# W' = w3 · w_out in three float32r passes instead of float32, its depth sum cut in two, and all float64 chunks converted by three VectorE operations

## The chip, the cores and the metric

One core of a Trainium2 chip. The metric is the device time of one execution in microseconds, the median of several runs. Engines: PE (TensorE, matmuls; PEld its weight loads), DVE (VectorE), ACT (ScalarE), POOL (GpSimd), SP (SyncE, which only issues DMAs here). Each works through its own queue in order.

## What is computed

Clustered attention over 2 x 8 heads of 768 x 64: a query sees only the keys whose nearest centroid is the same. Two MLPs follow on the 1536 x 512 result.

```python
scores = np.where(mask, scale * np.matmul(q, k.transpose(0, 1, 3, 2)), -1000000000.0)
attn = np.exp(scores - np.max(scores, axis=-1, keepdims=True))
attn = attn / (np.sum(attn, axis=-1, keepdims=True) + 1e-09)
x = np.matmul(attn, v)                                   # then to 1536 x 512
h = x @ w_in                                             # 512 x 2048
x = np.where(h >= 1, h, np.where(h <= -1, 0, (h + 1) ** 2 / 4)) @ w_out
out = ((x @ w1) * (x @ w2) @ w3) @ w_out2                # w1, w2 512 x 1024; w3 1024 x 1024; w_out2 1024 x 512
```

All weights arrive as float64. Because nothing stands between the last two products, the kernel makes W' = w3 @ w_out2 (1024 x 512) once, beside the attention, and multiplies by W'.

## The kernel before, in words

**Order.** Every step is registered with `add` (name, engines that can take it, planned cost, function, needs). ORDER is a string of letter pairs; each is the number of a step and which of its engines takes it, and the steps are emitted in that order. "takes", "frees", planned costs and due times were used when the string was made; at run time they emit nothing.

**Course.** Attention of batch 0 runs beside W' and the conversion of the first weights (to about 200 us); then the MoE products of batch 0 beside the attention of batch 1 (to about 470 us); then the products of batch 1. One score tile goes through PE (L855, two products in float32r), DVE (maximum, L863), POOL (scale, L868), ACT (exp, L876), PE (transpose, L893), ACT or DVE (copy to `pt`). Four PSUM tiles `sc` serve this in batch 0, `av` holds a PV product, and one bank `mo` serves W' and the transposes of the reciprocals (L950). Score tiles and head pairs are counted from 0.

**Chunks.** A weight chunk is 128 x 512. `chunk` (L1093) loads its float64 words (`w64`), and builds a float32 in a buffer `wf` (a ring of four): ACT takes the absolute of the high words (L1110), DVE clamps (L1114); then, in every second chunk (`by_add`), DVE shifts (L1136) and puts sign and top bits back (L1142), ACT rounds the low words (L1148), and POOL adds them (L1152). In the others ACT scales the low words by another form (L1120), and DVE ors them in while shifting (L1124) and ors the sign (L1130): three DVE operations, none on POOL. A chunk used by a float32r product is split into high and low halves: `whi` (ACT or DVE, L348 or L350), `wlo` (POOL or DVE, L353). 72 chunks are float64: 8 of w_out2, 16 of w3, and 48 that are also kept in DRAM (`wd`) for batch 1. The first 40 are all of w_out2 and w3 and 16 of the rest.

**W'.** For each of eight row blocks m and both halves hf of the depth, `wp_mm` (L1208) multiplies a w3 chunk, straight from `wf` in float32, by four blocks of `wo2` (float32, in SBUF), both halves into the one `mo` bank (L1212). After the second half `wp_copy` takes the bank to a `wf` buffer, and `wp_put` to DRAM. The eight steps with hf = 0 and those with hf = 1 alternate.

Of the kernel before, what the change touches and what calls it, by code (L numbers as in the profile page):

```python
# [38 lines left out]
    "###%$V$.$2$0#*#,#0$X$4$]$Z%s%X%Z#.:m%V#(#2%c#4$6%r%e%k$_$H%|%h:|&#&%$8$:$a%y%_&,#m#L;.%]$<$>$q$c%m$@$J$D$e$F"  # L39
    "%a#6#a#e#P;<%u:o$s$g#Z$i$B$L$k#F;H%i:q%o$m:s)u$N:w:u%w#:$#:y#V#H#8;#;()w#g#c$o$u#_#i#@#X;0#y)y)|;8#u#w$w#B*#"  # L40
    "#q;X*%$P;%#>$y$|;*;,;2;R;>$R$T*(**#R#o;g#]*4*,%#&*;B;4*.;_&)$,#T;6;@;:*6;J*@*B#s$%;Z*0;i*8#N*:;L;N*L#|;k*D*F"
    "*<;D#k;m*2;F*>*H#<;]#J#D*N;u;q*X;o*P*J$($**Z;a*R*]*u<(*_+(*T;P;T;w;c;e*a*W;|*c*e*g+4*w<6*m<*;s<B+*<2&0*y+6+,"
    "*|&5&3<R&>+.;y<,+8+:<.<#+L+#<8<%+0<<+<+%<:&7*i+2+@<0*k<D+X+B<4;V<T+N<e+D<X*o+P+F+Z+R*r+]&/+_+H+T*s+>&=+J+V+u"
    "+a+e<V<><F<H+c,4&:<Z,(+w&8<g+m,*+y<u<o<@,,+|,6<i<J,8,:,#<],.<k<_,L<L<N<m,&=*&F<|,0,<,@+g<P,B=:<q<w,N,2,P<y,>"
    "=#=%,D,R,X&H=L<b,F<c,u,w=,=(+i+k%>=.,Z,H,T=]%%<s,]%(,y=0=4=2=@=6,_,|,a,K,W=V-#+o=<=N=>=B-4&c=Q-(+r-%=k,c=8-*"
    "-,-6&D=c=|=_+s-8-:=D=a=e-.=R&U-@&@&B=F-0-<=g=i=I,e&L,m-2-B-D=J&N-?&K,g-F,i&R&Y=u=T&W>(=m-H-X,l=X,o=o-L-K&P&_"
    "-N-P-Z=Z>4>D>R-R-],r=q=s&e-_&^-u=w>>%B>#-w-T-a&b-y>c-V>%=y>J>*-|.#,s>6-d>,>8>F>T>.-e.(>]-g>:-m.*>u.%&k>H.,>L"
    "..>N>V>X><>0&g-i&[>2>@.4%*>P.@-l.L.6%@?,>Z.8>i.0>B.B.D.:.N>_.2&n&r.P&i.F.<.R&u-o>e?%.X.Z.H>a>w.]?:>y>|._&p?#"
    "?(-q.J?J.>>q.T.V>g>k>m>s.u.a?2/4.w?.>o/(&y?0?*?]/6.c.y.|&|/*(%()?m/,&w/@/#/./0($(-?P?D-s?<?4%,.m%D/B?>?L?_?@"
    "/8/:/<?a?6.e?8.g?N?R/%%./2?T/>?c?V?B%F%0?o?s?|%2?g/D?F?H/F/H@2?q%4(*?e%H?i%J?X/L?u/J?Z.i/N/X@D.k&s%L/P?k@,/Z"  # L50
    "/R/T%6/]?w%N@#/_?y@T(.@&.o.r%8/a/V/c%P.s@c@8%:@(/u@*@4/m%<%R%T@.@F@V@s/w/y/e(4@6@:@N0(@<04@H/|0#@JA,@>0608@Z"
    "0@@L@00*0:0,@P0&0B0.000D@m0<@A/g/i0F0LA<0H@X@]@e03@_0X/k@g@a@B0N@R0>@i0P0J0Z/o@kAJ0R0]0u@yA60T0w@u@o@qA.@w0y"
    "A>@|0|/r0_AB0a0WA#A%A@ALAD0cAFAH(01(/s(20eA0AZ1#1L0g1*0m1,1.10ANAP1NA2AT1%ARAVA4A(A*(612A81416180iF4FP1@Aa0l"
    "1X(81:1PA:1Z1B1]1_1D0o(;1<(=1FA]1H1RAmA_AX(>Ac1J(EAe(BAg1>(A1e1g(M(H1TAi0q1a1W(NAk1i1c2*(GAo0sB21kAq1u2,(J1m"
    "BP1w2.201y1|(P(Z22(RB424B61o2#2%1r1s26(T2(Bo(VAsAuAw(X282:BRBTB%B(Ay2F(]B82<2H2JC42>2A2LBc2BB+B,B:A|B=2DBr2N"
    "BDB#2PCRCqBeB>2RBg2TB/B1C7F>BsC(C9BFBiFkB@BH2cBB2V2XBV2eBJ2g2ZC*BM2]2_C-BuBk2iBNCU2aBm2kC.BXCV3%3(2mBZBw3*D%"
    "C0B]2oByC:34D4B|B_BaCFC<363,C$C&CtCXC33.C>Cu30DBCHC@3238D(D*3BCJCe3:CL3D3FCZDP3=3HCw3>Cg3@3P(a(`D7C]D93RCBCD"
    "2yCi3JC_Ck3L3N3T3V(g(c2qC|3XCyCNCQCnD,3_(e3Z3]DE3mD.D#DFDoCp3a(i3o3cE42s(t3q3eD>D@ER(l(u(m3s3gD:D<3i3u2uD04>"
# [1728 lines left out]
```

## Time and profile before

| | us |
|---|---|
| median of 3 runs (lowest to highest) | 735.21 (732.62 to 736.18) |
| the profiled execution's own time | 729.0 |
| its span, first to last instruction | 727.3 |
| PE busy in it | 706.3 |
| DVE busy in it | 620.3 |
| ACT busy in it | 467.9 |
| POOL busy in it | 308.2 |

The profile is of one execution, and its time need not be the median of the others. Busy shares are averages over stages that work differently, so the stretches of the attention, which has all engines at work, are to be read by themselves. An instruction's duration contains its start-up, which overlaps the one ahead of it: on a full queue the distance from start to start is shorter.

### The profile page before, as it was taken

The numbers are of one execution on the slowest core, as the hardware profiler recorded it, in microseconds if no ns is written. First come the engines' busy times: TensorE is split into PE (matmuls) and PEld (weight loads), VectorE is DVE, ScalarE is ACT, GpSimd is POOL, SyncE is SP. The second block draws the span as 40 slices with busy tenths as digits, with TensorE's granted clock in tenths as the row PEclk, the third lists the DMA queues.
The fourth block names the chain that finished last, engine by engine and source line by source line (L and its number), as shares of the span: only waits on it lengthen the run. The fifth ranks groups of instructions, "written<-read, shape, count | busy, mean of one in ns | idle before, by whom it ended". The sixth has DMA issues, their size and how long they took to land.

```text
span 727.3 us, 11952 instructions
## 1 busy us (share of the span) xinstructions
PE 706.3 (97%) x4120; PEld 620.5 (85%) x4121; DVE 620.3 (85%) x1120; ACT 467.9 (64%) x872; POOL 308.2 (42%) x371
## 2 busy tenths in 40 slices
...
GB/s 297 119 205 135 252 202 228 178 271 118 223 236 147 187 181 230 213 228 244 165 242 216 228 244 157 189 185 132 56 74 89 44 73 59 73 59 73 59 64 80
DMA packets 120204, 117.37 MB, mean 161 GB/s; under 512 B 80400, under 2 KB 89040, under 8 KB 120144
## 3 DMA queue, kind: packets, MB, share of 16 engines
...
q8 instruction: 32, 0.52, 0.3%
...
## 4 chain that ended last, share of the span: by engine, by line
PE 86%; DVE 5%; DMA 4%; ACT 3%; issue 2%; POOL 0%; ACTq 0%; POOLq 0%; DVEq 0%
PE mo L1268 34%; PE sc L1521 9%; PE sc L855 8%; PE mo L1212 6%; PE sc L1268 6%; PE mo L1521 6%; PE sc L893 4%; PE av L964 4%; PE av L972 3%; PE av L1521 2%; PE av L1268 2%; DMA vn<-phl 1%; DMA pt<-phl 1%; DMA wd<-wf 1%; DVE nm L863 1%
## 5 line engine op out<-in xcount | busy, mean ns | idle before, releaser
L1268 PE MATMUL mo<-X,whl 128*128 128x384 f32 x912 | 168.0, 338 | 0.0
L1268 PEld LDWEIGHTS mo<-X,whl 128*128 128x128 f32 x912 | 158.6, 188 | 2.5 <-issue 0.9
L1268 PE MATMUL mo<-G,whl 128*128 128x384 f32 x696 | 129.1, 340 | 0.8 <-DVE X L353 0.8
L1268 PEld LDWEIGHTS mo<-G,whl 128*128 128x128 f32 x696 | 122.3, 188 | 2.8 <-DVE X L353 1.1
L863 DVE TENSOR_REDUCE nm<-sc 128x1 f32<-128x768 f32 x96 | 90.1, 951 | 17.3 <-PE sc L855 13.1
L353 POOL TENSOR_TENSOR whl<-wf,whl 128x512 fp32r<-128x512 f32 x50 | 65.4, 1309 | 60.0 <-ACT whl L348 35.6
L1152 POOL TENSOR_TENSOR wf<-wf,w 128x512 int32<-128x512 int32 x32 | 45.0, 1408 | 56.9 <-DVE wf L1142 18.1
L868 POOL TENSOR_SCALAR nm<-nm 128x1 f32<-128x1 f32 x96 | 29.7, 310 | 92.0 <-DVE nm L863 88.7
L348 ACT ACTIVATE whl<-wf 128x512 fp32r<-128x512 f32 x71 | 44.6, 628 | 29.0 <-PE mo L1268 10.0
L855 PE MATMUL sc<-k,q 128*128 128x512 f32 (+1 forms) x192 | 54.8, 367 | 4.0 <-DVE kq L586 1.4
L1212 PE MATMUL mo<-wo,wf 128*128 128x512 f32 x128 | 57.9, 595 | 0.0
L876 ACT ACTIVATE sc<-sc,nm 128x768 f32<-128x768 f32 x44 | 38.3, 870 | 26.4 <-POOL nm L868 25.3
L876 ACT ACTIVATE P<-sc,nm 128x768 f32<-128x768 f32 x52 | 46.4, 896 | 13.0 <-DVE nm L863 7.0
L855 PE MATMUL sc<-kq 80*128 80x512 f32 (+1 forms) x192 | 49.4, 338 | 0.0
L353 DVE TENSOR_TENSOR phl<-sc,phl 128x768 f16<-128x768 f32 x44 | 41.8, 951 | 8.2 <-ACT phl L348 7.9
L893 PEld LDWEIGHTS sc<-ident,P 128*128 128x128 f32 x312 | 35.3, 140 | 12.2 <-ACT P L876 3.6
L1110 ACT ACTIVATE wf<-w 128x512 f32<-128x512 f32 x64 | 41.6, 671 | 4.2 <-POOL whl L353 2.3
L1212 PEld LDWEIGHTS mo<-wo,wf 128*128 128x128 f32 x128 | 23.3, 190 | 24.0 <-issue 23.0
L893 PE MATMUL sc<-ident,P 128*128 128x128 f32 x312 | 41.2, 274 | 1.8 <-ACT P L876 1.0
L855 PEld LDWEIGHTS sc<-k,q 128*128 128x128 f32 x192 | 31.4, 189 | 11.9 <-issue 3.9
L353 POOL TENSOR_TENSOR wh<-ws,wh 128x256 fp32r<-128x256 f32 x42 | 31.3, 758 | 17.8 <-DVE wh L350 9.6
L348 ACT ACTIVATE pt<-sc 128x768 f32<-128x768 f32 (+1 forms) x40 | 31.8, 811 | 9.7 <-PE sc L893 7.4
(242 smaller groups left out, 1546.4 us busy)
## 6 DMA issues: line engine op xcount, KB each, us to landing
...
```

The lines of the kernel that those rows point to most:

```text
L348: nc.scalar.activation(out=out, in_=in_, func=AF.Copy)
L353: (nc.gpsimd if e == "POOL" else nc.vector).tensor_tensor(out=out, in0=a, in1=b, op=ALU.subtract)
L855: nc.tensor.matmul(ps[:, n], q[0:n_rows, q0:q0 + 128], k[0:n_rows, n], start=first, stop=not first)
L863: nc.vector.tensor_reduce(out=nm, in_=T[("sc", b), s], axis=AX.X, op=ALU.max, negate=True)
L868: nc.gpsimd.tensor_scalar(out=tl[s, "nm"], in0=tl[s, "nm"], scalar1=SCALE, scalar2=EC, op0=ALU.mult, op1=ALU.add)
L876: nc.scalar.activation(out=new(("P", b), s).rearrange("p n s -> p (n s)") if by_pe(s) else T[("sc", b), s], in_=T[("sc", b), s], func=AF.E ...
L893: nc.tensor.transpose(T[("sc", b), s][:, c], p[:, c], ident)
L1110: nc.scalar.activation(out=T["wf", i], in_=T[w64, i].bitcast(F32)[:, :, 1], func=AF.Abs, scale=1.0 if by_add else float(2.0 ** 16))
L1152: nc.gpsimd.tensor_tensor(out=w, in0=w, in1=T[w64, i].bitcast(I32)[:, :, 0], op=ALU.add)
L1212: nc.tensor.matmul(acc, w[:, k4 * 128:(k4 + 1) * 128], wo2[:, hf * 4 + k4], start=(hf == 0 and k4 == 0), stop=(hf == 1 and k4 == 3),)
L1268: nc.tensor.matmul(acc, w[:, a, k4 * 128:(k4 + 1) * 128], rhs(c, k4), start=(first and k4 == 0 and n == 0), stop=(last and k4 == 3 and n = ...
L1521: nc.tensor.matmul(ps, lhs(av, a, k), rhs(bv, c, k), start=k == 0 and n == 0, stop=k == 1 and n == 2,)
```

## The change

- W' is made of high and low halves in float32r, three passes (high x high, high x low, low x high), as the other products are. So the 8 chunks of w_out2 and the 16 of w3 are split (24 `whi`, 24 `wlo`).
- The depth sum is cut in two: all eight first halves come first. `wp_part` copies each from the bank to a `wf` buffer, `wp_keep` writes it to DRAM (`wp0`), `wp_back` reads it again, and `wp_add` (DVE) adds the second half from the bank; `wp_put` is as before.
- Of the split w_out2 blocks six lie in four buffers, two of which are used twice; blocks 0 and 1 lie in the part of `X0` that the outputs of head pairs 2 and 3 fill later.
- `by_add` is False: all 72 float64 chunks take the three DVE operations, and POOL's addition is gone from 36 of them (20 of the first 40).
- ORDER is new, with some steps given to another engine.

The diff without the ORDER strings and some unchanged lines:

```diff
     down = const.tile([128, 1], F32, name="down")
+    wp0 = dram.tile([KF2, 128, DM], F32, name="wp0")
     wp = dram.tile([DM // 128, 128, KF2, 128], F32, name="wp")
...
     kq0 = early_p.tile([128, 2, NP, S], F32, name="kq0")
-    wo2 = early_p.tile([128, KF2, DM], F32, name="wo2")
+    BUFS["wo2"] = [early_p.tile([128, 2, DM], F32R, name=f"wo2{i}") for i in range(KF2 // 2)]
+    RINGS["wo2"] = KF2 // 2
+    BUFS["wo2x"] = [X0[:, :, j, :DM] for j in (KD - 1, KD - 2)]
+    RINGS["wo2x"] = 2
     late = {}
...
         "c_load": ((0.45, 0.18),), "al": ROWS, "ul": ROWS, "vl": ROWS, "ap": ROWS, "vT": ((0.62, 2.7),),
-        "sT": ((0.62, 2.7),), "k2": ROW * 2 + MASK, "wps": ((0.45, 1.05),), "wd": ((0.45, 1.05),),
+        "sT": ((0.62, 2.7),), "k2": ROW * 2 + MASK, "wps": ((0.45, 1.05),), "wps0": ((0.45, 1.05),), "wpl": ((0.45, 1.05),), "wd": ((0.45, 1.05),),
         "xs": ROW, "xr": ROW, "os": ROW,
...
                     [(("sc", b), s)],
-                    [((x, b), (u, h)) for x in ("k1", "q1", "kq2")] if t == NQ - 1 and g == NG - 1 else [],
+                    [((x, b), (u, h)) for x in ("k1", "q1", "kq2")],
                     near=(("sc", b), s),
...
                 ("pv", u, g), {"PE": 4.1 if whole(u) else 3.13}, p, pv(u, g), [("vT", u)] + [("sT", s + r) for r in range(NS)],
-                [("av", (u, g))], [("pt", (u, g, 0)), ("pt", (u, g, 1))] + ([("vn", u)] if g == NG - 1 else []), near=("av", (u, g)),
+                [("av", (u, g))], [("pt", (u, g, 0)), ("pt", (u, g, 1)), ("vn", u)], near=("av", (u, g)),
             )
...
             if b == 0:
-                add_split("x", nm, p + 3.5, lambda a, j=j, g=g: X0[:, a, j, cols(g)], [("xm", u, g)], "av", (u, g))
+                add_split("x", nm, p + 3.5, lambda a, j=j, g=g: X0[:, a, j, cols(g)], [("xm", u, g)] + ([("wp", m, 0) for m in range(KF2)] if j >= KD - 2 else []), "av", (u, g))
             else:
...
     nchunk = [0]
-    N_EARLY = 2 * KF2 + wo2.shape[1] + AHEAD
+    N_EARLY = 3 * KF2 + AHEAD
     c64 = []
...
-    def chunk(t, src, is64, split=True, dst=None, needs=(), keep=None):
+    def chunk(t, src, is64, split=True, halves="whl", needs=(), keep=None):
         i = nchunk[0]
...
         w64 = ("w64", 0 if i < N_EARLY else 1)
-        by_add = low_by_pool(i)
+        by_add = False
...
         def absv(e):
-            if dst is None:
-                new("wf", i)
-            else:
-                T["wf", i] = dst
+            new("wf", i)
             nc.scalar.activation(out=T["wf", i], in_=T[w64, i].bitcast(F32)[:, :, 1], func=AF.Abs, scale=1.0 if by_add else float(2.0 ** 16))
...
         def hi(e):
-            copy(e, new("whl", i)[:, 0], T["wf", i])
+            copy(e, new(halves, i)[:, 0], T["wf", i])
...
         def lo(e):
-            w = T["whl", i]
+            w = T[halves, i]
             sub(e, w[:, 1], T["wf", i], f(w)[:, 0])
...
             add(("wl", i), {"ACT": 0.2}, t - 14.0, load, list(needs) + W_AFTER[i:i + 1], [(w64, i)], behind="w64", moves=((0.46, 1.8),))
-            add(("wabs", i), {"ACT": 0.56}, t - 9.0, absv, [("wl", i)], [] if dst is not None else [("wf", i)], behind="wf")
+            add(("wabs", i), {"ACT": 0.56}, t - 9.0, absv, [("wl", i)], [("wf", i)], behind="wf")
             add(("wc", i, 0), {"DVE": 0.34, "POOL": (1.92, LATE)}, t - 8.6, clamp, [("wabs", i)])
...
         if split:
-            add(("whi", i), {"ACT": 0.52, "DVE": (0.34, LATE)}, t - 5.0, hi, [last], [("whl", i)], behind="whl")
+            add(("whi", i), {"ACT": 0.52, "DVE": (0.34, LATE)}, t - 5.0, hi, [last], [(halves, i)], behind=halves)
             add(("wlo", i), {"POOL": 1.3, "DVE": (0.61, LATE)}, t - 4.0, lo, [("whi", i)], frees=[("wf", i)])
...
-    W_ACC = [("mo", 0), "av", ("sc", 0), ("sc", 0)][:W_SIDE] + [("mo", 0)] * (KF2 - W_SIDE)
-
-    def wp_acc(m, first=False):
-        ring, name = W_ACC[m], ("wp", m)
-        t = new(ring, name) if first else T[ring, name]
-        if ring == ("sc", 0):
-            o = 0 if where[ring, name] % PER[0] == 0 else S - 512
-            t = t[:, o:o + 512]
-        return t
-
-    def wp_mm(i, m, hf):
-        def fn(e):
-            w = T["wf", i]
-            acc = wp_acc(m, hf == 0)
+    def wo2_home(kt):
+        return "wo2x" if kt < 2 else "wo2"
+
+    def wp_mm(i, m, hf, x):
+        def fn(e):
+            w, acc = T["whl", i], new(("mo", 0), ("wp", m, hf))
             for k4 in range(4):
-                nc.tensor.matmul(
-                    acc, w[:, k4 * 128:(k4 + 1) * 128], wo2[:, hf * 4 + k4],
-                    start=(hf == 0 and k4 == 0), stop=(hf == 1 and k4 == 3),
-                )
-        return fn
-
-    def wp_copy(m):
-        def fn(e):
-            copy(e, new("wf", ("wp", m)), wp_acc(m))
+                for n, (a, c) in enumerate(PASSES):
+                    nc.tensor.matmul(
+                        acc, w[:, a, k4 * 128:(k4 + 1) * 128], T[wo2_home(hf * 4 + k4), x[k4]][:, c],
+                        start=(k4 == 0 and n == 0), stop=(k4 == 3 and n == 2),
+                    )
+        return fn
+
+    def wp_part(m):
+        def fn(e):
+            copy(e, new("wf", ("wp0", m)), T[("mo", 0), ("wp", m, 0)])
+        return fn
+
+    def wp_keep(m):
+        def fn(e):
+            nc.sync.dma_start(out=wp0[m], in_=T["wf", ("wp0", m)])
+        return fn
+
+    def wp_back(m):
+        def fn(e):
+            nc.sync.dma_start(out=new("wf", ("wp", m)), in_=wp0[m])
+        return fn
+
+    def wp_add(m):
+        def fn(e):
+            w = T["wf", ("wp", m)]
+            nc.vector.tensor_tensor(out=w, in0=w, in1=T[("mo", 0), ("wp", m, 1)], op=ALU.add)
         return fn
...
     wo2_chunks = []
-    steps = [(m, hf) for hf in range(2) for m in range(W_SIDE)] + [(m, hf) for m in range(W_SIDE, KF2) for hf in range(2)]
+    WO2_AT = {0: range(4), 3: (4,), 5: (5,), 8: (6, 7)}
+    steps = [(m, hf) for hf in range(2) for m in range(KF2)]
     for n, (m, hf) in enumerate(steps):
         t = T_W + dt * n
-        if m == 0:
-            for kt in range(hf * 4, hf * 4 + 4):
-                wo2_chunks.append(chunk(t - 10.0 + 2.0 * (kt % 4), w_out2[kt], True, False, wo2[:, kt]))
-        i = chunk(t, w3T[m, hf], True, False)
-        needs = [("wc", i, 3)] + [("wc", x, 3) for x in wo2_chunks[hf * 4:hf * 4 + 4]]
-        if hf:
-            needs.append(("wp", m, 0))
-        elif W_ACC[m] == ("sc", 0):
-            needs.append(("am", 0, "q", NP - 1))
+        for kt in WO2_AT.get(n, ()):
+            wo2_chunks.append(chunk(t - 10.0 + 2.0 * (kt % 4), w_out2[kt], True, True, wo2_home(kt)))
+        x = wo2_chunks[hf * 4:hf * 4 + 4]
+        i = chunk(t, w3T[m, hf], True, True)
+        acc = (("mo", 0), ("wp", m, hf))
         add(
-            ("wp", m, hf), {"PE": 3.44}, t, wp_mm(i, m, hf), needs,
-            [(W_ACC[m], ("wp", m))] if hf == 0 else [], [("wf", i)],
+            ("wp", m, hf), {"PE": 2.8}, t, wp_mm(i, m, hf, x), [("wlo", i)] + [("wlo", y) for y in x],
+            [acc], [("whl", i)] + [(wo2_home(hf * 4 + k4), y) for k4, y in enumerate(x)],
         )
...
             chunk(t + dt / 2, src, True, False, keep=x)
-        if hf:
-            add(
-                ("wpe", m), {"ACT": 0.5, "DVE": (0.61, LATE)}, t + dt, wp_copy(m), [("wp", m, 1)],
-                [("wf", ("wp", m))], [(W_ACC[m], ("wp", m))],
-            )
+        if hf == 0:
+            add(("wpe0", m), {"ACT": 0.5, "DVE": (0.61, LATE)}, t + dt, wp_part(m), [("wp", m, 0)], [("wf", ("wp0", m))], [acc])
+            add(("wps0", m), {"DMA": 0.5}, t + dt + 2.0, wp_keep(m), [("wpe0", m)], frees=[("wf", ("wp0", m))])
+        else:
+            add(("wpl", m), {"DMA": 0.5}, t - 4.0, wp_back(m), [("wps0", m)], [("wf", ("wp", m))])
+            add(("wpe", m), {"DVE": 0.61}, t + dt, wp_add(m), [("wp", m, 1), ("wpl", m)], frees=[acc])
             add(("wps", m), {"DMA": 0.5}, t + dt + 2.0, wp_put(m), [("wpe", m)], frees=[("wf", ("wp", m))])
```

## Rows read from the trace of the kernel before

**Rows 1.** The page, part 1: engine, busy us (share of the span), instructions.

```profile
PE 706.3 (97%) x4120; PEld 620.5 (85%) x4121; DVE 620.3 (85%) x1120; ACT 467.9 (64%) x872; POOL 308.2 (42%) x371
```

**Rows 2.** Stretches: from:to, length, busy (count) by engine, PEclk, DMA share, GB/s.

```profile
0.00:64.65 64.65, 50.65 (x321) 35.53 (x322) 57.05 (x106) 54.59 (x89) 20.88 (x37) 1.00 0.54 186
64.65:123.22 58.57, 58.57 (x299) 37.84 (x299) 53.17 (x85) 47.01 (x82) 27.93 (x31) 1.00 0.66 224
123.22:201.55 78.33, 76.29 (x397) 44.38 (x397) 68.16 (x110) 58.61 (x101) 24.39 (x37) 1.00 0.64 201
201.55:364.50 162.95, 162.62 (x1003) 153.62 (x1002) 145.78 (x248) 130.99 (x242) 79.03 (x91) 1.00 0.90 203
...
477.00:727.30 250.30, 246.82 (x1402) 245.43 (x1400) 196.86 (x410) 105.83 (x233) 109.26 (x125) 1.00 0.27 81
20.00:60.00 40.00, 37.00 (x235) 28.44 (x237) 37.57 (x67) 35.61 (x62) 10.85 (x18) 1.00 0.41 138
```

**Rows 3.** Chain of work that ended last: start us, us, what.

```profile
51.80 3.44 PE mo L1212 x8
...
203.67 0.71 PE sc L855 x4
204.37 2.09 PE mo L1268 x12
```

**Rows 4.** Timeline of DVE, 33 to 41: start us, us, engine, line, operation, operands.

```profile
33.53 0.42 DVE L1114 TENSOR_SCALAR wo<-wo 128x512 f32<-128x512 f32 x1
33.86 0.68 DVE L1124 SCALAR_TENSOR_TENSOR wo<-wo,w 128x512 uint32<-128x512 uint32 x1
34.47 0.42 DVE L1136 TENSOR_SCALAR wo<-wo 128x512 uint32<-128x512 uint32 x1
34.80 0.68 DVE L1130 SCALAR_TENSOR_TENSOR wo<-w,wo 128x512 uint32<-128x512 uint32 x1
35.40 0.42 DVE L1114 TENSOR_SCALAR wf<-wf 128x512 f32<-128x512 f32 x1
```

**Rows 5.** Lines by shape, 0 to 201.55: operation xcount | busy, mean ns | idle before, releasers.

```profile
L1152 POOL TENSOR_TENSOR wf<-wf,w 128x512 int32<-128x512 int32 x16 | 22.6, 1417 | 21.3 <-DVE wf L1142 9.4 <-ACT pt L348 4.2 <-PE av L964 3.0
...
L1120 ACT ACTIVATE w<-w,down 128x512 uint32<-128x512 uint32 x20 | 15.5, 775 | 3.4 <-POOL wf L1152 2.3 <-ACT P L876 0.6 <-issue 0.5
L1148 ACT ACTIVATE w<-w 128x512 uint32<-128x512 uint32 x20 | 13.7, 685 | 1.8 <-DVE wo L1136 1.0 <-issue 0.8
...
L348 ACT ACTIVATE pt<-sc 128x768 f32<-128x768 f32 x37 | 29.3, 810 | 7.3 <-PE sc L893 5.0 <-PE sc L855 1.9
L350 DVE COPY pt<-sc 128x768 f32<-128x768 f32 x11 | 10.4, 951 | 0.8 <-PE sc L893 0.7
...
L353 POOL TENSOR_TENSOR whl<-wf,whl 128x512 fp32r<-128x512 f32 x2 | 2.6, 1286 | 2.0 <-ACT whl L348 2.0
L350 DVE COPY wf<-mo 128x512 f32<-128x512 f32 x3 | 2.1, 686 | 1.8 <-DMA wd<-wf 1.8
L348 ACT ACTIVATE whl<-wf 128x512 fp32r<-128x512 f32 x2 | 1.3, 632 | 0.0
```

**Rows 6.** Lines by shape, 201.55 to 364.5: both halves of a chunk on DVE.

```profile
L353 DVE TENSOR_TENSOR whl<-wf,whl 128x512 fp32r<-128x512 f32 x11 | 7.5, 683 | 1.8 <-ACT whl L348 1.7
L350 DVE CAST whl<-wf 128x512 fp32r<-128x512 f32 x10 | 4.7, 472 | 0.0
```

**Rows 7.** Waits of PE, 123.22 to 201.55 and 201.55 to 364.5: total us, times, longest.

```profile
PE mo L950 <- DVE wf L350: 0.7, 1, 0.7
...
PE sc L855 <- DVE phl L353: 0.3, 1, 0.3
```

**Rows 8.** Line 1124 alone: duration ns min/median/max, first and last start.

```profile
L1124 DVE SCALAR_TENSOR_TENSOR wf<-wf,w x32: 675/691/1676, 38.5 to 449.6; 128x512 uint32<-128x512 uint32 x32
```

More of the change, by code (lines that the diff above doesn't have):

```diff
@@ L38 @@
 ORDER = (
[L39 to L58, printed above, removed]
@@ new lines @@
+    ";L#s*L*H*N*P*X#Z*Z*];V;X;i;N;k&&;o;Q;q*J$,#H#u*u;s*R*T+4&>*_*e;|<#*g;R*a*V*c+(+**w+6;];_*m<%<(<*<2&.+,*y&0&:"
+    "*|+@+.+#+&+8+:+<<D<4<6;a;c<V+0+2+>+L&3*i*k<i+B+D+N+P+X+Z+]*o<8<:&7&5<<<>+F+R&G*q+_<F<H<-+e<.*s<y;e;v&K+H+T+u"
+    "+a+J+V+c,(+w,4,6,*<J&8&<&I<]<X<k+m+y+|,#,L,8,:,,,.=2=%<Z<_<L<m&M<N<Q<R;w%>%(<a<c,0,%,2,@,B,D,X&N,N&D<o<q=D,<"
+    ",>,Z<s<0<A<|=V,F<B=#=(,u,P,R+g+i+l=*,T,H+o=8,],_,a<u<w=i=4,J,V,w,y,|+r=J=6,e=:=<=,=.=>&Q<T<f<g-#-%,c&@-(-*+s"
+    "-4-6=y=o>2=F=H-,-.&C-8,g=L=X=Z&c-:&j=0=@=B=N=]=_=a=c-0-2=P=R=k-@,i-<-L-B-D-X-Z-]>%&T>D-N-P=|>#=m&_-F->>(=q=s"
@@ new lines @@
+    ">V&k>4,k=u=w>8>i>*>,>.>6-R&X,m,o-H-u-K-w,r-y>:&S><>>=T=e=g>|-T,s%%.(.*%@-_>J>F-V>H>X>Z>L>]-|>_&W>a>c>N>0-a&e"
+    "-c?4>@>k&o>B.#-e&^.4.6>m&a&[%*>Q.%>o>q>S>s&n?D.,..?(-m&s-g-i-k?:>u>w.8.0.@.B.D.3-o>T>f>g.L.N?T?#?%?*?6?8&g?,"
+    "?.?<?F?H-q.:&u?g.F.X.<.P.R.T?J?Z?>?|?V.H.Z.J?L.W?X@4.>?N.]._>y?@?0.u?2.a?m.c%B?]?Q/4/(?_?a?C?S/@/6-s.w/B/*@H"
+    "&y(&?u?c?e?w?y&q@Z(#@(?i&w(-%,@#?k@%&|?o(((.%D/8.y.|@6@8@*.e/:?q?s/,/./D@,@:@<.m@J@L@>@@/#/%@N@P@R/</0/2@o/>"
+    "%.%0%2%4@.@0/F@T@V/L%F%H.g/N/P%6%J/H@BA(A<@a@]@`/J@u@i@2AN@D%L(*%8/R@q@F/X/Z(4.i.k/]%:.o@c@s%<%N@e@g/_/e@w/g"
```

85 lines of the change are left out of this document (48 added, 37 removed).

## Prediction

> **What bounds the kernel now.** I read the page's busy shares first, then a table of stretches, then the chain of work that ended last, and the lines by duration only after that. The shares put PE at 97% and DVE at 85% [rows 1]; as averages they hide where a second engine is close. The stretches [rows 2] are cut at events of the PE sequence: score tile 16 (64.65), about score tile 32 (123.22), and the first MoE matmul (201.55). In the second, 64.65 to 123.22, PE is busy for all of its 58.57 us, but DVE is busy for 53.17 of them and ACT for 47.01. In the third DVE has 68.16 of 78.33. From 201.55 on PE is busy for 162.62 of 162.95, and so on to the end. PE is the bound everywhere after the start-up, with DVE 9% behind it in the second stretch. The granted clock is 1.00 in every stretch, so it plays no part.
>
> The chain shows what PE spends on W': one half step (eight recorded matmuls, float32) takes 3.44 us on the path [rows 3], and there are 16. The first starts at 51.80 and the last is over before 201.55, in the stretches where DVE and ACT are nearly full. That is the question: PE work is removed where PE's neighbours have least room.
>
> **PE.** A half step becomes 12 float32r matmuls of 512 columns, 6144 columns. Twelve of 384 (4608) take 2.09 us, and a score tile of 2 x (512 + 256) = 1536 takes 0.71 [rows 3]: 0.454 to 0.462 ns a column, so 2.79 to 2.84 us; I take 2.80, as the chunk matmuls have the same weights and passes. Saved: 16 x (3.44 - 2.80) = 10.2 us. By the new order 7 of the 16 lie between score tiles 16 and 32 as before, and one more score tile (0.71) stands ahead of the first MoE matmul. PE alone would reach that at 201.55 - 10.2 + 0.7 = 192.0.
>
> **VectorE ahead of the first MoE matmul.** On a full queue the step from start to start counts, not the duration: clamp 33.53 to 33.86 = 0.33, shift-or 0.61, mask-shift 0.33, sign-or 0.60 [rows 4], each 0.07 to 0.09 under its duration. I decoded both orders into steps and counted them per engine up to this point.
> - 20 of the 40 early float64 chunks used clamp, rebase, top (0.33 + 0.33 + 0.60 = 1.26) and a GpSimd addition. Now clamp, shift, sign: 0.33 + 0.61 + 0.60 = 1.54. Added: 20 x 0.28 = 5.6.
> - The 24 chunks of W' are now split. 9 high halves go to DVE at 0.472 - 0.08 = 0.39, and 5 low halves at 0.683 - 0.08 = 0.60 [rows 6]: 3.5 + 3.0.
> - Evictions of W' on DVE go from 3 to 12 (4 copies of first halves, 8 additions). The copy is 0.686 - 0.08 = 0.61 [rows 5]. The 512-wide addition from PSUM isn't in the trace; it lies between that and the 768-wide copy's 0.951 - 0.08 = 0.87, and I take 0.61, the same number of columns: 9 x 0.61 = 5.5 (upper end 7.6).
> - The order takes work off DVE: six 768-wide copies of transposed probabilities go to ACT and two other 768-wide ones come back, 4 x 0.87 = 3.5 less; and a net seven smaller q, k and X steps go, at 0.39 to 0.87 each, 4.2 less (2.7 to 6.1).
>
> Sum: 17.6 - 7.7 = +9.9 us. By their places, about -2.4 up to score tile 16, +7.2 to tile 32, +4.9 behind. So DVE has 54.6, then 53.17 + 7.2 = 60.4, then 73; PE has 64.0, then 58.57 - 7 x 0.64 = 54.1, then 78.33 - 9 x 0.64 + 0.7 = 73.3. **In the middle stretch DVE passes PE by 6 us, and behind it the two are level.**
>
> **ScalarE and GpSimd there.** ACT: 15 more high halves at 0.632 - 0.09 = 0.54 (8.1), four more 768-wide copies at 0.72 (2.9) [rows 5], about six smaller ones (3.8), one eviction less (-0.5), and 20 roundings of the other form at 0.775 instead of 0.685 (1.8) [rows 5]: +16.1 on the 54.59 + 47.01 + 58.61 = 160.2 of rows 2, so 176 of some 197, beside its DMA issues. Not the bound alone, but its idle time, which used to soak up DVE's and PE's jitter, halves. GpSimd loses 20 additions of 1.417 and gains 19 subtractions of 1.286 [rows 5]: -28.3 + 24.4, flat. The chunk's chain no longer ends on POOL, but a W' step now starts from POOL's low half instead. If POOL were late by one subtraction, PE would wait 1.3.
>
> **What waits anew.** The first halves leave the one "mo" bank by a copy, so it is handed over 16 times instead of 8, each time through ACT's or DVE's queue, with a W' step or a reciprocal transpose behind it on PE. The order puts at least two other PE groups (0.66 + 0.7) between most neighbours, about what the 0.69 eviction needs if its queue is free. Before, such a handover cost PE one wait of 0.7 in the third stretch [rows 7]. Bounds: nothing, and 8 more x 0.7 = 5.6; I take 1, inside the DVE idle below. The first halves go to DRAM and back: eight writes and eight reads of 256 KB, 4 MB where the DMA share is 0.54 to 0.66 [rows 2], and the reads are issued a step ahead; I take 0 for them. A late read would hold the DVE addition, the score maxima queued behind it, and the bank. They also take buffers of "wf", which has four; a full ring would hold ACT's queue at the next Abs. The outputs of head pairs 2 and 3 wait for all eight first halves, which the order has finished before that pair's first PV product: 0. The "takes" and "frees" of the planner emit nothing.
>
> **A rule on the shared port.** One shift-or of 32 took 1676 ns, but the median, 691, is within 16 ns of the fastest [rows 8], although POOL is busy for 31 to 48% of the stretches up to the first MoE matmul [rows 2]. The Trainium skill (SBUF — State Buffer, "SBUF: two separate sides") says that DVE and GpSimd take a shared port pair as an exclusive lock, also when the DVE operation has two SBUF inputs and the GpSimd one reads SBUF, and that the later one fully blocks. If that held for each meeting, the added two-input operations would pay, and that is a rival below.
>
> **From 201.55 on.** The later 16 affected chunks add 16 x 0.28 = 4.5 to DVE, and the order shifts about as much again to it between the first MoE matmul and the a/b products: 145.78 + 10 of 163, 96%, while PE waited 0.3 there before [rows 2, 7]. I charge 1 us (0 to 3), and take off the 0.7 of the score tile moved forward. The last 250 us have DVE at 196.86 of 250.3: no change.
>
> **The sum.** DVE's queue: 178.4 + 9.9 = 188.3, plus the 7.6 that it idles in the first stretch (64.65 - 57.05), is 195.9 without any further idle. With 2% idle behind tile 16, 62.3 + 133.4 / 0.98 = 198.4. I take the middle, 197.1, 4.4 earlier than 201.55. What follows takes 727.3 - 201.55 = 525.75 now, and 525.75 - 0.7 + 1 = 526.0 then: span 197.1 + 526.0 = 723.1. The profiled execution's own time is 729.0, 1.7 over its span, so 724.8, which is 4.2 less. The median of the runs is 735.21, 6.2 above that execution; I carry the difference: 735.2 - 4.2 = 731.0.
>
> **Rivals.**
> - PE stays the bound: the DVE and ACT queues run ahead through the first stretch, and DVE work that isn't needed by the first MoE matmul lags past it. For: from 20 to 60 us DVE was already busy for 37.57 of 40, 94% [rows 2], and what it did there for the chunks waited on nothing of PE. Against: +7.2 in the middle stretch. Arrival 192 to 194, time 726 (725 to 728).
> - The gain is eaten up: DVE idle of 3 to 4.5% behind tile 16, arrival 200 to 201.5: 735 (733.5 to 736.5).
> - Slower, by DVE in the middle stretch: every score tile goes PE, DVE, POOL, ACT, PE, and the four PSUM score tiles let little run ahead; with bank handovers and "wf" in the same queue, DVE doesn't get under 3.7% idle. That is the point from which it decides (133.4 / 0.963 + 62.3 = 200.8, no gain left). Before, it idled 5.4 of 58.57, 9%, as PE was the bound. At 6%: 62.3 + 141.9 = 204.2, 3.4 late, time 738 to 739; the full 9% would give 743.
> - Slower, by the port: 25 more two-input operations, a POOL instruction in progress at 38% of them, 1676 - 691 = 0.98 each: 9.3 us on DVE, arrival near 205, time 739. The rows speak against it: half of the 32 are within 16 ns of the fastest.
>
> **How the numbers follow.** Forecast (729 to 733.5) 0.42; PE stays the bound 0.22; eaten up 0.17; slower by DVE 0.15; slower by the port 0.04. A measurement of this kernel can tell about 0.5% from no change, 3.7 us, so faster is under 731.5 and slower over 738.9. Faster: 0.22 and a good half of the forecast, 0.46. Slower: two thirds of the two slower cases, 0.14. Same: 0.40. The range leaves out the fastest third of the PE case and the worst of the slow ones: 725 to 739; for the forecast alone it is 729 to 733.5.
>
> **What would show it.** W' steps of 2.8 us on PE. The first MoE matmul at 195 to 199 us. DVE busy for 96% or more between score tiles 16 and 32 and PE waiting there by several us in sum, on scores, on transposes behind ACT, or on "mo"; were PE gapless there, the second reading would be right. After the first MoE matmul PE gapless within 2 us. The forecast is wrong if "wf" or the bank holds a queue for more than single microseconds, or if ACT and not DVE is the late one.

## The result, and the profile after

| | before | after |
|---|---|---|
| median (lowest to highest) | 735.36 (732.62 to 736.18) | 725.43 (723.67 to 726.57) |
| ratio of after to before, 95% interval | | 0.9869 [0.9836, 0.9903] |
| profiled execution, its span | 729.0, 727.3 | 726.57, 724.9 |

The change is faster by 9.9 us, 1.3%. The forecast was 731.0, a gain of 4.2, with 725 to 739 as its range. The two profiled executions differ by only 2.4 us, so most of the 9.9 isn't in that pair of traces at all. Where it is was the question for the experiments.

The page of after, part 1, answers [rows 1]: engine, busy us (share of the span), instructions.

```profile
PE 700.6 (97%) x4184; PEld 632.5 (87%) x4185; DVE 631.0 (87%) x1135; ACT 482.9 (67%) x897; POOL 283.4 (39%) x351
```

Over the span DVE is busy for 10.7 us more, ACT for 15.0 more, POOL for 24.8 less, PE for 5.7 less as recorded. By the first MoE matmul it is 3.8 more for DVE and 16.5 for ACT, where the forecast had 9.9 and 16.1; behind it 6.9 more for DVE, where the forecast had 4.5 and "about as much again". The stretches of after, cut at the same points of PE's sequence as in [rows 2] (the 16th score tile, the end of the 33rd, the first MoE matmul), with the same columns:

```profile
0.00:63.67 63.67, 50.75 (x325) 35.66 (x326) 53.74 (x101) 54.96 (x89) 23.88 (x39) 1.00 0.56 193
63.67:123.57 59.90, 57.30 (x327) 44.42 (x327) 57.51 (x96) 55.56 (x98) 20.76 (x27) 0.97 0.71 229
123.57:198.77 75.20, 72.03 (x433) 50.51 (x433) 70.97 (x115) 66.19 (x111) 27.89 (x38) 1.00 0.77 243
198.77:361.70 162.93, 161.57 (x996) 152.88 (x996) 150.58 (x248) 129.07 (x238) 64.96 (x81) 1.00 0.91 212
```

The first MoE matmul comes at 198.77 instead of 201.55. In the second stretch PE is no longer busy throughout (57.30 of 59.90), and DVE (57.51) and ACT (55.56) are near it; the stretch is no shorter than before (58.57). The granted clock is 0.97 there: it fell to 0.66 in one slice of 5 us, behind a wait of PE, as this table by slices shows.

```profile
110.00:115.00 5.00, 3.58 (x20) 2.54 (x18) 4.96 (x10) 5.00 (x12) 2.81 (x5) 1.00 0.67 209
115.00:120.00 5.00, 4.99 (x21) 4.54 (x22) 4.32 (x8) 4.05 (x7) 0.57 (x1) 0.66 0.74 240
```

So after's profiled execution has one small disturbance of its own. From the first MoE matmul to the end of the span it takes 526.1 us; before took 525.75.

### The profile page after: what moved, and what is told of

It reads as the page before. It is cut to its first block, busy times and chain, and to the rows that moved or that the text cites. A ratio compares the mean times of both kernels' runs of the same rounds, so it can differ in the third digit from the quotient of the medians.

```text
span 724.9 us, 12096 instructions
## 1 busy us (share of the span) xinstructions
PE 700.6 (97%) x4184; PEld 632.5 (87%) x4185; DVE 631.0 (87%) x1135; ACT 482.9 (67%) x897; POOL 283.4 (39%) x351
## 4 chain that ended last, share of the span: by engine, by line
PE 74%; DVE 6%; ACT 3%; issue 2%; DMA 0%; POOL 0%; DVEq 0%; SPq 0%; ACTq 0%; POOLq 0%
PE mo L1277 36%; PE sc L1277 7%; PE sc L1530 6%; PE sc L860 6%; PE mo L1530 5%; PE mo L1207 3%; PE av L977 3%; PE sc L898 2%; PE av L1277 2%; PE av L969 2%; PE av L1530 2%; ACT pt L353 1%; DVE wf L1132 1%; DVE tv L1441 1%; ACT P L881 1%
## 5 line engine op out<-in xcount | busy, mean ns | idle before, releaser
L358 POOL TENSOR_TENSOR whl<-wf,whl 128x512 fp32r<-128x512 f32 x64 | 86.1, 1346 | 113.5 <-ACT whl L353 79.6
L1277 PE MATMUL mo<-G,whl 128*128 128x384 f32 x660 | 122.5, 340 | 0.2 <-DVE G L358 0.2
L1277 PEld LDWEIGHTS mo<-G,whl 128*128 128x128 f32 x660 | 116.0, 188 | 1.9 <-issue 0.6
L353 ACT ACTIVATE whl<-wf 128x512 fp32r<-128x512 f32 x84 | 52.5, 628 | 46.6 <-PE mo L1277 19.6
L1122 ACT ACTIVATE w<-w,down 128x512 uint32<-128x512 uint32 x72 | 54.8, 768 | 0.4 <-ACT whl L353 0.3
L1112 ACT ACTIVATE wf<-w 128x512 f32<-128x512 f32 x72 | 47.9, 672 | 6.8 <-POOL whl L358 2.6
L1132 DVE SCALAR_TENSOR_TENSOR wf<-w,wf 128x512 uint32<-128x512 uint32 x72 | 51.6, 721 | 0.8
L1126 DVE SCALAR_TENSOR_TENSOR wf<-wf,w 128x512 uint32<-128x512 uint32 x72 | 50.0, 698 | 2.2 <-ACT w L1122 1.0
L1277 PE MATMUL sc<-G,whl 128*128 128x384 f32 x240 | 43.7, 339 | 0.0
L1277 PEld LDWEIGHTS sc<-G,whl 128*128 128x128 f32 x240 | 42.5, 188 | 0.0
```

Source lines behind the costliest of these rows:

```text
L353: nc.scalar.activation(out=out, in_=in_, func=AF.Copy)
L358: (nc.gpsimd if e == "POOL" else nc.vector).tensor_tensor(out=out, in0=a, in1=b, op=ALU.subtract)
L1112: nc.scalar.activation(out=T["wf", i], in_=T[w64, i].bitcast(F32)[:, :, 1], func=AF.Abs, scale=1.0 if by_add else float(2.0 ** 16))
L1122: nc.scalar.activation(out=lo, in_=lo, func=AF.Identity, scale=float(2.0 ** -29 - 2.0 ** -41), bias=down)
L1126: nc.vector.scalar_tensor_tensor(out=w, in0=w, scalar=3, in1=T[w64, i][:, :, 0], op0=ALU.logical_shift_left, op1=ALU.bitwise_or)
L1132: nc.vector.scalar_tensor_tensor(out=w, in0=T[w64, i][:, :, 1], scalar=0x80000000, in1=w, op0=ALU.bitwise_and, op1=ALU.bitwise_or)
```

## The experiments

The theories when they began. **A**: DVE holds the stretch up to the first MoE matmul, as the prediction says, and the gain is what is left. **B**: PE stays the bound there. **C**: ACT, the second full queue, holds it. **D**, formed after the first runs: before loses time in most executions somewhere else, and the new order doesn't. Each kernel ran beside runs of before; a ratio is to those. The arrival of the first MoE matmul is read off the chain for the two repeats, like the 201.55 of the prediction; for the changed kernels behind them it is read off PE's timeline, where before again has it at 201.30 and after again at 196.29, and differences go by those two.

**Before again.** No edit.

> The kernel before once more, unchanged, to learn how its executions differ among themselves: the profiled one took 729.0, the timed ones 732.6 to 736.2. If the profiled one was a lucky execution (theory S: a spread that comes from the attention stretch up to the first MoE matmul), this profile is near 735, and the first MoE matmul starts 4 to 7 us after 201.6. If the profile is shorter as such (theory P), it is near 729 again with that start at 201 to 202, and the timed runs are near 735.

Measured: 734.3 (729.7 to 736.43), ratio 1.0015 [0.9984, 1.0046]. The finding is how the executions of before stand to their clock. Of 65 in three sets of runs, 16 have a mean granted clock of 0.999 or more, with a median of 729.3 (727.42 to 730.83); 18 have 0.997 or 0.998, with a median of 732.3; 31 have less, with a median of 734.7 (732.19 to 736.54). The execution of [rows 1] (729.0) was one of the first kind, and this one's profile (736.43) one of the last. Its first MoE matmul is at 201.54, as there (201.55), so the difference arises behind it. Stretches of 5 us in it, columns as in [rows 2]:

```profile
360.00:365.00 5.00, 5.00 (x31) 5.00 (x30) 3.30 (x9) 2.50 (x5) 2.69 (x3) 1.00 1.20 100
365.00:370.00 5.00, 1.20 (x7) 0.88 (x5) 0.00 (x0) 0.61 (x1) 0.81 (x2) 1.00 1.35 126
370.00:375.00 5.00, 3.61 (x10) 3.01 (x11) 4.77 (x8) 2.83 (x7) 1.65 (x3) 0.55 0.73 182
375.00:380.00 5.00, 5.00 (x25) 5.00 (x23) 3.85 (x8) 4.76 (x9) 0.79 (x1) 0.77 0.71 237
```

All compute engines stand nearly still from 365 to 370, and then PE's granted clock is 0.55 and 0.77. The chain of the same execution (start us, us, what) names the cause:

```profile
354.93 0.32 PE mo L1268 x2
355.24 14.07 DMA vn<-phl
...
369.39 0.82 ACT phl L348
370.21 0.02 issue
370.23 0.96 DVE phl L353
...
373.04 8.53 PE mo L1268 x36
```

A DMA transpose of v (line 774, head pair 6) takes 14.07 us. ACT's next copy needs the buffer that the transpose reads and waits 6.9; DVE's half behind it and PE's next score tile wait on that (PE 5.0). Then 36 MoE matmuls take 8.53 at the lower clock; with two loads less (below) 36 take 6.36 to 6.54. In the 729.0 execution of before the same piece is:

```profile
354.86 8.78 DMA vn<-phl
```

There ACT waited 1.9 and PE 0.8. What stands beside it, from ACT's timeline of this run: two loads of 512 KB each, issued 1.55 us apart, around the transpose's issue at 355.24.

```profile
354.26 0.33 ACTq L1101 DMA_DIRECT2D w<-in_w_dram  x1
...
355.81 0.36 ACTq L1101 DMA_DIRECT2D w<-in_w_dram  x1
```

**After again.** No edit.

> The changed kernel once more, unchanged. Theory S expects the same spread of some us as in the four executions so far (723.7 to 726.6) and a ratio of 0.983 to 0.990 to the kernel before. A profile of this run without the half clock at 115 to 118.5 us would be 1.5 to 2 us shorter up to the first MoE matmul, at about 197.

Measured: 724.85 (724.1 to 725.41), ratio 0.9876 [0.9854, 0.9898], every execution at a clock of 1.0. The first MoE matmul is at 196.46, 5.1 earlier than before, and the rest takes 722.7 - 196.46 = 526.2. The transpose of v for head pair 6 is issued at 343.87 here, the loads of 512 KB around it at 342.47, 349.21 and 354.72; the four such transposes land after 4.0 to 6.4 us, and from 355 to 380 PE is busy in all 25 us. Stretches up to the first MoE matmul, and PE's waits from 20 to 200 (total us, times, longest):

```profile
65.00:125.00 60.00, 57.37 (x331) 43.73 (x329) 58.60 (x96) 56.89 (x98) 24.14 (x31) 1.00 0.75 243
125.00:196.00 71.00, 67.98 (x416) 47.46 (x416) 66.75 (x111) 62.02 (x106) 24.56 (x35) 1.00 0.76 237
```

```profile
PE sc L898 <- ACT P L881: 3.0, 5, 1.1
PE sc L860 <- ACT pt L353: 2.7, 7, 0.6
PE sc L860 <- ACT P L881: 1.2, 2, 0.9
PE mo L955 <- DVE wf L1231: 0.6, 2, 0.4
```

The second and third stretch between the points of [rows 2]:

```profile
62.65:121.08 58.43, 55.83 (x327) 42.75 (x327) 56.95 (x96) 55.40 (x98) 20.74 (x27) 1.00 0.73 235
121.08:196.46 75.38, 72.03 (x433) 50.49 (x433) 71.13 (x116) 66.26 (x111) 28.02 (x38) 1.00 0.77 242
```

The second is as long as before (58.57); the 5.1 come from the first (62.65 for 64.65) and the third (75.38 for 78.33). From 65 to 125 DVE is busy for 58.60 of 60 (97.7%). PE's waits are short and many, on score tiles that ACT still has to read or transform; the "mo" bank (last line of the waits) costs 0.6.

**Before without two of its loads.** This tests D. The loads of chunks 73 and 74 are left out (their weights are then what the buffer held):

```diff
         def load(e):
+            if i in (73, 74):
+                new(w64, i)
+                return
```

> The kernel before without the loads of float64 chunks 73 and 74 (left out: these chunks hold an older chunk's words), the two 512 KB loads issued about the DMA transpose of v for head pair 6, at 354 to 356 us. In one execution that transpose landed after 8.8 us and the time was 729.0; in another after 14.1, ACT's copy waited 6.9 for it, PE 5.0, PE's clock fell to its lower level at 370 to 380, and the time was 736.4. If the shared DMA engines make that wait (theory D), the transpose lands in 5 to 7 us, no execution is above 731, and the median is 726 to 729. If the spread has another source (theory S), it stays 727 to 736 with a median of 732 to 734.

Measured: 727.91 (727.41 to 729.28, 10 runs, nine of them at a clock of 0.999 or 1.000), ratio 0.9944 [0.9921, 0.9968]. The spread of 9 us is gone. From 355 to 380, where the 729.0 execution of before had PE idle for 0.83 us, PE is busy throughout; three of the five slices:

```profile
360.00:365.00 5.00, 5.00 (x30) 4.96 (x29) 4.95 (x10) 3.52 (x7) 3.87 (x5) 1.00 0.56 145
365.00:370.00 5.00, 5.00 (x29) 4.71 (x28) 4.44 (x10) 3.52 (x8) 1.16 (x2) 1.00 0.99 246
370.00:375.00 5.00, 5.00 (x31) 4.66 (x31) 4.41 (x8) 3.86 (x7) 2.83 (x3) 1.00 0.82 235
```

D is shown for before: the meeting of transpose and loads makes its spread and most of the distance from 728 to its median. Its first MoE matmul is at 200.80, 0.5 earlier.

**After with a load moved to the transpose.** The ACT load of chunk 73 is put right behind the v transpose of head pair 6; only ORDER differs.

> The changed kernel with one step moved in its order: the 512 KB load of float64 chunk 73 is issued right behind the DMA transpose of v for head pair 6 (about 344.5 us) and not 5 us later. If a load beside that transpose makes the wait (theory D), the transpose lands 2 to 8 us later than the 4 to 6.4 measured, and some executions are up to 8 us longer, the median 726 to 730. If the kernel before lost its time there for another reason, nothing changes: 724 to 726.

Measured: 724.84 (723.47 to 728.11), ratio 0.9902 [0.9868, 0.9936]; the median is that of after, though four of the ten executions take 727.2 to 728.1, for which no cause was looked for. The transpose was issued at 348.19, the loads at 346.78 and 350.35: 2.2 us behind it where before has 0.6. It landed in 5.1 us, and the buffer's next user comes about 10 us later in this order. The stall was not made in after, so how close the loads have to come, and whether it takes more than them, is open. One load close behind is not enough: the v transpose at 269.67 of after again has one 0.57 behind it, the other 6.42 ahead, and lands after 6.41.

**The passes undone.** W' from float32 products, 4 per half step (8 recorded matmuls) instead of 12 in three passes; they take the low halves alone, so the product is another; the splits stay:

```diff
-                for n, (a, c) in enumerate(PASSES):
-                    nc.tensor.matmul(
-                        acc, w[:, a, k4 * 128:(k4 + 1) * 128], T[wo2_home(hf * 4 + k4), x[k4]][:, c],
-                        start=(k4 == 0 and n == 0), stop=(k4 == 3 and n == 2),
-                    )
+                nc.tensor.matmul(
+                    acc, f(w)[:, 1, k4 * 128:(k4 + 1) * 128], f(T[wo2_home(hf * 4 + k4), x[k4]])[:, 1],
+                    start=k4 == 0, stop=k4 == 3,
+                )
```

> The changed kernel with each W' half step as four float32 products of the low halves (left out: the other products, so W' is not the reference's) instead of twelve float32r ones; everything on DVE, ACT, POOL and the queues stays. PE gets its 16 x 0.64 = 10.2 us back. If PE holds the bound of that stretch in the changed kernel (rival 'PE stays the bound'), the time rises by 8 to 10 us to 733 to 735. If DVE holds it (the forecast's step), PE's extra work fits partly into its gaps, and the time rises by 3 to 6.

Measured: 734.59 (732.1 to 737.45), ratio 1.0028 [0.9997, 1.0059]. The first MoE matmul is at 205.0, 8.7 behind after's; this profile (736.64) is 3.5 longer behind that matmul too, which the edit doesn't explain, so the arrival says more than the time. The half steps take 3.44 again, from the chains of this kernel and of after's second run:

```profile
142.97 3.44 PE mo L1206 x8
```

```profile
155.12 2.80 PE mo L1207 x12
```

So 8.7 of the 10.2 us by which the float32 products are longer on PE appear in the arrival: PE counts in that stretch, as B has it, though not as a gapless bound (2.63 us idle of 60 above).

**DVE relieved.** The clamp of the early chunks is left out (38 operations, 12.5 us of DVE at 0.33 each; the lowest weights aren't clamped):

```diff
         def clamp(e):
+            if i < N_EARLY:
+                return
```

> The changed kernel without the clamp of the first 40 chunks (left out: the limits for values that do not occur in these inputs): 38 operations less on DVE, 0.33 each, 12.5 us, all before the first MoE matmul. If DVE holds the bound there, it falls by 3 to 6 us, until PE's 192 is reached. If PE holds it, it falls by less than 1.5.

Measured: 725.73 (723.19 to 727.64), ratio 0.9886 [0.9854, 0.9919]; first MoE matmul at 197.09, 0.8 later. DVE is busy for 13.1 us less up to there and falls to 53.10 of 60 between 65 and 125, and nothing is gained. (The granted clock is 0.97 in that stretch; it is 1.00 in the run with both edits below.) Theory A, that DVE's own work alone sets the pace, falls.

**ACT relieved.** The scaling of the low words is left out for the early chunks (40 operations, 26 us of ACT at 0.65 each; their low halves are masked away):

```diff
         def low_floor(e):
+            if i < N_EARLY:
+                return
```

> The changed kernel without ACT's scaling of the low words in the first 40 chunks (left out: the low words enter wrongly): 40 operations of 0.65 us, 26 us less on ACT before the first MoE matmul; DVE, PE and POOL have the same work. PE saved 10.2 us, but that matmul came only 2.8 to 5.1 earlier, and PE's waits there name ACT. If ACT's queue holds back the rest, the start comes at 192 to 194 and the time falls to 720 to 722. If it is the length of the chain of a score tile, or the start-up, it stays at 195.5 to 197 and the time at 724 to 725.

Measured: 726.68 (723.8 to 730.83), ratio 0.9928 [0.9899, 0.9958]; first MoE matmul at 199.11, 2.8 later, with ACT at 47.61 of 60 from 65 to 125. Theory C falls as well.

**Both relieved.** Both edits at once.

> The changed kernel without the clamps (DVE, 12.5 us less) and without the scaling of low words (ACT, 26 us less) in the first 40 chunks (left out: both, so the low words enter wrongly). Either cut alone left the first MoE matmul at 197 to 199 instead of 196.5. If DVE and ACT hold that stretch together, each full where the other is relieved, it comes at 192 to 194 now, and the time is 720 to 722. If neither queue holds it (the chain of a score tile through four PSUM tiles, or POOL), it stays at 195.5 to 199 and the time at 724 to 727.

Measured: 724.19 (722.95 to 727.86), ratio 0.9887 [0.9855, 0.9918]; first MoE matmul at 196.86. From 65 to 125 neither neighbour is full, and PE still isn't:

```profile
65.00:125.00 60.00, 57.55 (x333) 43.61 (x333) 55.46 (x82) 48.28 (x84) 23.35 (x31) 1.00 0.74 248
```

PE waits some 9 us from 20 to 205 here as well, mostly on ACT's copies and exponentials. The load of these two queues isn't what keeps PE from 192.

**DVE burdened.** The early clamps are done twice:

```diff
-            (nc.gpsimd if e == "POOL" else nc.vector).tensor_scalar(
+            for _ in range(2 if i < N_EARLY else 1):
+                (nc.gpsimd if e == "POOL" else nc.vector).tensor_scalar(
```

> The changed kernel with the clamp of the first 40 chunks done twice (nothing else differs): 38 operations of 0.33, 12.5 us more on DVE, all before the first MoE matmul, 10 to 11 of them where DVE is busy for 94 to 98%. If DVE is full there, the time rises by 8 to 12 to 733 to 737. If it still has the room that the run without clamps suggests (no change when 12.5 us were taken away), it rises by less than 4.

Measured: 745.27 (741.94 to 748.11), ratio 1.0167 [1.0101, 1.0232]. The time is above both of the expected ranges. The first MoE matmul is at 216.28, 20.0 later than in after. The plan counted the added work at 12.5 us, 0.33 for each of 38 operations, and that price was too low here: up to that point DVE is busy for 203.43, where after again has 182.47, so 21.0 more, and the clamps alone take 35.9 instead of 16.7.

```profile
0.00:216.28 216.28, 183.81 (x1082) 130.52 (x1084) 203.43 (x349) 177.22 (x296) 77.30 (x106) 0.98 0.62 205
L1117 DVE TENSOR_SCALAR wf<-wf 128x512 f32<-128x512 f32 x76 | 35.9, 476 | 1.4
```

PE's waits from 20 to 220 grow, and the clock falls behind the longest of them (3.3 us in 145 to 160):

```profile
PE sc L898 <- ACT P L881: 9.1, 9, 3.3
```

```profile
145.00:150.00 5.00, 2.33 (x20) 0.96 (x20) 4.90 (x7) 0.81 (x2) 1.82 (x1) 0.99 0.82 282
150.00:155.00 5.00, 4.37 (x14) 3.70 (x15) 4.87 (x6) 4.82 (x10) 3.51 (x4) 0.50 0.84 309
```

DVE work taken away gains nothing, DVE work added comes back in the arrival (20.0 for 21.0), part of it by way of the lower clock. DVE is at its limit without being the only limit.

**One part alone: the three operations.** Before, with by_add False and its own order (the new operations at the old ones' places).

```diff
-        by_add = low_by_pool(i)
+        by_add = False
```

> The kernel before, in its own order, with only the conversion changed: all 72 chunks take three DVE operations, POOL adds nothing, W' stays float32. DVE gets 20 x 0.28 = 5.6 us more before the first MoE matmul and 10 in all, POOL 51 less. If DVE's load decides (the step of the forecast), the first MoE matmul comes 2 to 4 us later, at 204 to 206, and the time rises by that. If PE holds that stretch with room on DVE, the start stays within 1 us of 201.6 and the time at 732 to 735, with the same spread as before (727.6 to 736.5).

Measured: 746.96 (742.45 to 747.7), ratio 1.0197 [1.0142, 1.0251]; first MoE matmul at 209.72, 8.4 later than before and beyond both expectations, with PE waiting on DVE (3.4 on the sign operation alone, 2.1 on copies of "pt"). Behind that matmul it takes 536.3 where before took 525.75 and, in its long execution, 533.2: the v transpose of head pair 6, again between two loads (1.0 ahead, 0.5 behind), lands after 11.9, and PE's granted clock is 0.57 in the 5 us from 380.

**One part alone: W'.** After, with GpSimd's additions back at the places of the third operations.

```diff
-        by_add = False
+        by_add = low_by_pool(i)
```

> The changed kernel in its new order with only W' changed: every second chunk is put together with POOL's addition again. If the gain comes from W' and the new order, 724 to 727, first MoE matmul at 196 to 198. If the three operations were needed to let POOL take the 24 low halves (POOL then has 20 x 1.42 = 28 us more before that point, and low halves queue behind them), PE waits on POOL at W' steps by 3 to 8 us and the time is 728 to 733.

Measured: 762.15 (760.24 to 765.56), ratio 1.0422 [1.0368, 1.0477]; first MoE matmul at 223.32, and the time is far above the 728 to 733 of the worse expectation. PE's waits from 20 to 200:

```profile
PE mo L955 <- POOL tmp L945: 7.9, 2, 6.6
PE sc L898 <- ACT P L881: 6.3, 6, 1.7
PE sc L860 <- ACT P L881: 5.6, 3, 5.0
```

The reciprocal's tile from GpSimd, which now makes low halves of W' and the additions as well, comes up to 6.6 us late. Neither part is a gain by itself. Each stood in an order made for something else, so the runs don't tell what either would give in an order of its own.

## Why the prediction was right, and where its size was not

The sign and the range held. Of the mechanism PE's saving, ACT's growth and the stretch behind the first MoE matmul held, DVE's sum did not. The size was 4.2 against 9.9. The spans of the two repeated profiles, before's with the stall and after's without, split it:

| | before again | after again | earlier by |
|---|---|---|---|
| to the first MoE matmul | 201.54 | 196.46 | 5.1 |
| from there to the end | 533.2 | 526.2 | 7.0 |

- **The step that failed: the difference carried.** "The median of the runs is 735.21, 6.2 above that execution; I carry the difference". The profiled execution was one in which the transpose landed after 8.78 and cost PE 0.8; the one profiled later, near the top of the spread (736.43), has it at 14.07 and loses 5 us of waiting and about 3 of a lower clock (2.1 on the 36 matmuls, 1.1 on the score tile ahead of them, which took 1.79 from 371.25 to 373.04 instead of 0.70). The new order has the second load 5.3 us behind that transpose instead of 0.6, and none of after's profiles shows the stall: after's profiled and median times lie within 1.2 of each other. A difference between a profile and its median is a part of the kernel with a place, and an order that moves everything moves it too. The prediction noticed the 6.2 and asked nothing of it.
- **The gain it did work out** is there at its size. Executions of before at a clock of 0.999 or more have a median of 729.3, after's is 724.85: 4.5, for 4.2 forecast. Against before without the two loads (727.91) it is 3.1.
- **PE's half step**: 2.80 forecast; 2.79 to 2.83 measured in 12 of the 16 pieces that the chains of after's two profiles show, 2.99 to 3.21 in the other four. That they count almost in full is shown by the float32 run (+8.7 to the first MoE matmul for 10.2). (The prediction's "9 x 0.64" counts 17 half steps; with 8 in the last stretch PE has 73.9 there.)
- **The arrival**: 197.1 forecast (195 to 199); 196.46 and 198.77 measured. **DVE 96% or more** in the middle: 97.5% between the points of [rows 2]. But the sum behind 197.1 had DVE busy for 188.3 and idle for 8.8; measured are 182.5 and 14.0. Two errors of 5 to 6 us cancel, so that the arrival came out is in part luck.
- **Why it arrives there** was half right. "DVE passes PE by 6 us" and sets the pace: in the middle stretch DVE is 1.1 above PE (56.95 and 55.83), and DVE relieved of 13.1 us, ACT of some 25, or both, gains nothing that the runs can tell. Burdened, it costs at once. So PE with its waits and DVE with its own seem to lie at nearly the same length, where more on either counts (8.7 for 10.2 on PE, 20.0 for 21.0 on DVE) and less on DVE alone doesn't. PE alone was put at 192.0, and after again is 4.5 behind that. Before (first two lines) and after again, columns as in [rows 2]:

```profile
0.00:20.00 20.00, 8.99 (x57) 4.77 (x57) 14.83 (x33) 15.05 (x20) 9.12 (x16) 1.00 0.82 291
0.00:201.55 201.55, 185.51 (x1015) 117.75 (x1017) 178.38 (x299) 160.22 (x271) 73.20 (x104) 1.00 0.61 203
0.00:20.00 20.00, 12.56 (x69) 6.65 (x70) 14.29 (x36) 16.58 (x22) 8.39 (x16) 1.00 0.84 310
0.00:196.46 196.46, 179.73 (x1083) 129.78 (x1085) 182.47 (x311) 176.63 (x296) 72.65 (x104) 1.00 0.70 225
```

  Of the 4.5, 3.7 is busy time: PE's fell by 5.8 where 10.2 - 0.7 = 9.5 was counted. Only 0.7 is idle time, 16.7 instead of 16.0, but it moved: 3.6 less in the first 20 us, 4.3 more behind them. (Part of the 3.6 is no gain of the change: PE's first matmul comes at 7.4 in both profiles of before, but at 5.8 in the run without the two loads, whose start is the same.) Some of the busy time is at the start, which the change leaves alone (80 transposes of line 470 take 12.5 instead of 11.3, 32 products of line 540 take 6.3 instead of 5.2); the rest wasn't traced. The idle time behind the start is some 9 us of waits of up to 1.1 each, mostly on ACT, for the chain of a score tile (PE, DVE, POOL, ACT, PE) through four PSUM tiles; with both queues relieved it stays (16.8 in all), and no run took that chain apart.
- **VectorE's terms**: the 512-wide addition from PSUM, bounded by 0.61 and 0.87, took 683 ns, that of a 512-wide copy (686), so the lower end taken was right. Their sum was too high: DVE's busy time up to the first MoE matmul rose by 4.1, not 9.9. Of the 5.8 between them 2.6 are two steps at the start that the change doesn't touch and that were shorter in after again (lines 437 and, for 384 columns, 564 before, 442 and 569 after: 5.6 us against 3.0). **wp0, the "wf" ring and the bank**: PE waits for the "mo" bank for 0.8 where 1 was charged, and DVE's additions 0.9 in all for what is read back, which was put at 0.
- **From the first MoE matmul on**: 526.0 forecast, 526.2 and 526.1 measured.
- **The rivals.** "PE stays the bound" had the arrival at 192 to 194, which no run came to, but its mechanism counts: PE's work came back nearly in full. "Slower, by DVE" is what the doubled clamps make: the mechanism was real, 21 us of DVE further on. (In its sum 204.2 is 2.65 behind 201.55; the "3.4 late" counts from 200.8. In the one above it, 4.5% idle gives 202.0, not 201.5.) "The port" is there, but at few places: 67 of the 72 shift-ors of after again start with no POOL instruction in progress and take 651 to 709 ns, although POOL is busy for 24.14 of 60 us; three start inside its small scalings and take 683 to 695; the two that start inside a two-input operation of POOL end 0.55 behind its end and take 917 and 1331. The 1676 of [rows 8] is such a meeting, too (before, then after again; start us, us):

```profile
119.11 1.35 POOL L1152 TENSOR_TENSOR wf<-wf,w 128x512 int32<-128x512 int32 x1 [1.61 <-DVE wf L1142]
119.34 1.68 DVE L1124 SCALAR_TENSOR_TENSOR wf<-wf,w 128x512 uint32<-128x512 uint32 x1
444.70 1.20 POOL L358 TENSOR_TENSOR X<-tmp,X 128x384 fp32r<-128x384 f32 x1
445.12 1.33 DVE L1126 SCALAR_TENSOR_TENSOR wf<-wf,w 128x512 uint32<-128x512 uint32 x1
```

  The rule of the Trainium skill (SBUF — State Buffer, "SBUF: two separate sides"), by which the later of the two is blocked, agrees with these meetings. So the prediction's reading, that a median near the fastest speaks against the rule, was wrong: the median says how rare the meetings are. What the rival had wrong is their number, 38% of the operations; here 5 of 72 start inside a POOL instruction, 2 of them inside a two-input one. Why they are so rare wasn't looked into.
